# Batch 7's gate product in seven half-size products, and a new order of the work behind piece 340

## The chip, the cores and the metric

One core of one Trainium2 chip runs the whole program. The metric is the device time of one execution in microseconds. TensorE (PE, with its weight loads shown apart as PEld), VectorE (DVE), ScalarE (ACT) and GpSimd (POOL) each work through their own queue in order; SyncE (SP) issues the DMAs.

## What is computed

Per batch (8) and head (8) there are two attentions over 576 positions, one over means of four and one over a band of +-3, and their outputs are added. The 512-wide result x goes through a gated network:

```
h = gelu(x @ w_in)                     # 512 -> 1024
u, v = h[..., :512], h[..., 512:]
v_n = (v - mean) / sqrt(var + 1e-6) * g_ln
v_s = einsum('ts,bsd->btd', w_sg, v_n) + b_sg[None, :, None]
out = x + (u * v_s) @ w_out
```

## The kernel before

**Pieces and order.** The program is a list of small pieces, each with a name, the engines that can run it, what it comes after and which buffers it takes and gives back. The string ORDER names every piece in the order in which it is issued, with the engine behind a slash where there is a choice (A for ACT, V for DVE, P for POOL). So each engine's queue is written out by hand. `place` hands out the eight PSUM banks and the numbered SBUF buffers (10 of kind X, 38 of kind R) along that list; waits between engines follow from the data.

**Names.** The number behind an attention piece is the group g (batch x 4 + pair of heads, 0 to 31): YS scores, T, U and t the turning of probabilities, D the product with the values, xa, xb the merge, xh and xl the high and low part of x. In the network the first number is the batch: v7.3 is the third 128-position tile of the v half of batch 7 (12 matmuls; v7.4 is the left-over 64 positions, 8), vg its gelu, vb its statistics, vp the root on POOL, vn the normalising, vh and vl its high and low part. u is the other half (12 matmuls each), ua its gelu. s is the gate product, sa its scale and bias (DVE reads PSUM), sm the multiplication with u, ga to gd sums of gate blocks, gh and gl their high and low parts, o the out product, oa its addition to x, os the store.

**Numbers in two parts.** Each float32 operand is cut into a high part that the matmul takes exactly and a remainder. A product is three matmuls: high by high, low by high, high by low.

**The gate product before.** For each 128 columns of v_n and each half (288) of the output positions, `s_mm` adds 4 tiles of positions x 3 terms and 2 matmuls for the left-over 64, 14 in all; eight such pieces s7.0 to s7.7 make a batch. Each has a bank of its own and one sa reads it. From batch 1 on the out product is made with seven products of 6 matmuls instead of eight (`o_mm_s`, the Winograd form of Strassen's scheme), and several of them share a bank, which DVE reads in between.

**What ends the program.** The last pieces are out products of batch 7, their additions and eight half-block stores.

Of the kernel before, what the change touches and what calls it, by code (L numbers as in the profile page):

```python
# [1221 lines left out]
```

## Time and profile before

| | us |
|---|---|
| three timed runs | 565.53, 567.17, 568.70 (median 567.17) |
| the profiled execution | 564.37, its span 562.4 |
| PE busy | 546.4 (97%) |
| DVE, ACT, POOL busy | 437.2, 392.7, 364.1 |

The span runs from the first to the last instruction that the profiler saw. A matmul's end is modelled and matmuls overlap in the pipeline, so the mean length of one is longer than the distance to the next.

### The profile page before, as it was taken

To read this page: it belongs to the slowest core of one execution; us is meant where nothing else is said; L and a number is where in the kernel's file an instruction comes from. 1 tells how busy PE (TensorE), PEld (TensorE's weight loads), DVE (VectorE), ACT (ScalarE), POOL (GpSimd) and SP (SyncE) were. 2 spreads that over 40 slices of the span, in tenths; PEclk is the share of its full clock that TensorE was granted. 3 is DMA by queue.
4 is the path that set the end of the run, shared out by engine and by line. 5 is a ranking of instruction groups with operands and counts; after the bars stand their busy time and mean duration, and the time that the engine had idled before them with its cause. 6 is when DMAs were issued, how large, how long until landed. Compare 5 with 4: busy or idle time off the path is not lost.

```text
span 562.4 us, 17517 instructions
## 1 busy us (share of the span) xinstructions
PE 546.4 (97%) x6948; PEld 510.1 (91%) x6948; DVE 437.2 (78%) x929; ACT 392.7 (70%) x1302; POOL 364.1 (65%) x462
## 2 busy tenths in 40 slices
PE   6888999999999999999999999999999999999997
PEld 4677999799988999989999999989999899989997
DVE  7998899966889887796867867898669776565375
ACT  2897989779845989568987978377868588324310
POOL 6995987796776765747567645448655875655422
PEclk9998999999999999999999999999999999999999
DMA  8979551411623044041443124213353032200002
GB/s 290 289 237 339 196 179 40 121 45 37 204 82 121 23 140 157 16 153 55 135 124 105 46 83 152 77 55 105 108 172 102 11 113 78 99 1 0 32 34 105
DMA packets 31040, 62.72 MB, mean 112 GB/s; under 512 B 3696, under 2 KB 4720, under 8 KB 30960
## 3 DMA queue, kind: packets, MB, share of 16 engines
q1 hardware_dynamic: 30960, 61.62, 34.8%
q8 instruction: 54, 0.88, 0.7%
q14 instruction: 26, 0.21, 0.1%
...
## 4 chain that ended last, share of the span: by engine, by line
PE 79%; DVE 8%; ACT 4%; DMA 4%; POOL 3%; issue 2%; DVEq 0%; POOLq 0%; SPq 0%; ACTq 0%
PE ps L896 34%; PE ps L801 17%; PE ps L1019 14%; PE ps L677 3%; PE ps L693 2%; PE ps L616 2%; PE ps L625 2%; PE ps L514 2%; PE ps L535 2%; ACT X L574 2%; DMA R<-in_v_dram 2%; DMA R<-in_qT_dram 1%; DMA weight_z<-in_w_in_dram 1%; DVE vs L943 1%; POOL X L610 1%
## 5 line engine op out<-in xcount | busy, mean ns | idle before, releaser
L896 PE MATMUL ps<-wsg_h,R 128*128 128x288 f32 x576 | 122.6, 299 | 0.0
L896 PE MATMUL ps<-X,weight_z 128*128 128x288 f32 x512 | 110.8, 298 | 0.0
L801 PE MATMUL ps<-weight_y,X 128*128 128x512 f32 x320 | 98.1, 400 | 0.6 <-DVE vs L943 0.6
L574 ACT ACTIVATE X<-X,nb 128x64 f32<-128x64 f32 x280 | 93.6, 343 | 3.1 <-DVE nb L553 2.8
L896 PEld LDWEIGHTS ps<-wsg_h,R 128*128 128x128 f32 x576 | 93.8, 188 | 0.9
L896 PE MATMUL ps<-wsg_l,R 128*128 128x288 f32 x320 | 92.6, 295 | 0.0
L896 PEld LDWEIGHTS ps<-X,weight_z 128*128 128x128 f32 x512 | 84.6, 188 | 0.4
L896 PE MATMUL ps<-R,weight_z 128*128 128x288 f32 x256 | 75.4, 295 | 0.0
L801 PEld LDWEIGHTS ps<-weight_y,X 128*128 128x128 f32 x320 | 58.0, 189 | 12.4 <-DVE vs L943 1.2
L1026 DVE TENSOR_TENSOR R<-ps,R 128x288 f32<-128x288 f32 x98 | 43.0, 450 | 26.6 <-PE ps L1019 26.4
L896 PEld LDWEIGHTS ps<-wsg_l,R 128*128 128x128 f32 x320 | 60.3, 188 | 0.0
L244 ACT CAST R<-R 128x576 fp32r<-128x576 f32 (+2 forms) x65 | 41.5, 646 | 25.9 <-POOL R L949 10.1
L574 ACT ACTIVATION_READ_ACCUMULATOR X<-X,nb 128x1 f32 x280 | 54.5, 195 | 0.0
L1002 POOL TENSOR_TENSOR R<-R,R 128x576 fp32r<-128x576 f32 x23 | 35.2, 1531 | 27.5 <-ACT R L244 17.2
L949 POOL TENSOR_TENSOR R<-R,vs 128x288 f32<-128x288 f32 x29 | 24.8, 858 | 42.9 <-DVE vs L943 33.7
L1019 PE MATMUL ps<-R,weight_r 128*128 128x288 f32 x336 | 51.4, 297 | 0.0
L943 DVE SCALAR_TENSOR_TENSOR vs<-ps,g_sb,b_sb 128x288 f32<-128x288 f32 x64 | 32.5, 512 | 23.8 <-PE ps L896 20.9
L801 PE MATMUL ps<-weight_y,R 128*128 128x512 f32 x128 | 51.0, 398 | 0.0
L896 PEld LDWEIGHTS ps<-R,weight_z 128*128 128x128 f32 x256 | 48.2, 188 | 0.1
L1019 PEld LDWEIGHTS ps<-R,weight_r 128*128 128x128 f32 x336 | 46.8, 188 | 1.0
L498 POOL TENSOR_TENSOR pairs<-R 112x256 f32<-112x256 f32 x56 | 45.3, 809 | 3.3 <-DMA R<-in_v_dram 3.2
L244 ACT COPY R<-ps 112x288 f32<-112x288 f32 (+4 forms) x83 | 29.1, 391 | 17.6 <-PE ps L625 5.1
...
## 6 DMA issues: line engine op xcount, KB each, us to landing
...
```

The lines of the kernel that those rows point to most:

```text
L244: (nc.scalar.copy if e == "A" else ENG[e].tensor_copy)(**kw)
L498: ENG[e].tensor_tensor(out=pairs, in0=v[:, 0:2], in1=v[:, 2:4], op=ALU.add)
L514: nc.tensor.matmul(out=sp[i][os, c * KB:(c + 1) * KB], lhsT=q[hs, t * QB:t * QB + KB], rhs=k[hs, t * QB:t * QB + KB], start=not early, sto ...
L574: nc.scalar.activation(out=st["ms"][:, t, :], in_=src, func=AF.Exp, bias=st["nb"][:, t:t + 1], scale=scale, accum_out=sums[par][:, t:t + 1])
L677: nc.tensor.matmul(out=out, lhsT=lhsT, rhs=pdt[ks, probs, h * QC:(h + 1) * QC], start=first, stop=last)
L801: nc.tensor.matmul(out=acc, lhsT=r32(l), rhs=r32(weights[f"y{k}"][:, 0, w]), start=(i == 0 and ks[0] == 0), stop=(i == len(ops) - 1 and ks ...
L896: nc.tensor.matmul(out=acc[:, 0:HALF], lhsT=r32(l), rhs=r32(r), start=(first and n == 0), stop=(last and n == len(ops) - 1))
L943: nc.vector.scalar_tensor_tensor(out=vsb[i], in0=at["ps", "m", b, "s", i][:, 0:HALF], scalar=g_sb[:, i // 2:i // 2 + 1], in1=b_sb[:, half( ...
L949: ENG[e].tensor_tensor(out=gate(i), in0=gate(i), in1=vsb[i], op=ALU.mult)
L1002: ENG[e].tensor_tensor(out=r32(gl[m]), in0=us[raws[m]], in1=gh[m], op=ALU.subtract)
L1019: nc.tensor.matmul(out=bank(j, c), lhsT=r32(l), rhs=r32(r), start=first and i == 0, stop=i == len(ops) - 1, skip_group_check=not first)
L1026: nc.vector.tensor_tensor(out=x, in0=bank(j, c), in1=x, op=ALU.add)
```

## The change

The gate product of batch 7 (SMALL_S = 7) is made in the seven-product form too. The positions s are cut into two halves of two tiles, the columns of v_n into two halves of 256, the output positions into two halves of 288.

Weights: `gate_whole` adds the two parts of w_sg again (gf0 to gf4), `gate_combo` makes four differences of quarters (gx1 to gx4) and one of the left-over rows (gx5), `gate_split` cuts them into high (gy) and low (gz) parts. They go into six buffers of kind X (and a seventh for the left-over rows); the third overwrites the quarter of w_sg that no product uses any longer once the odd s pieces of batches 0 to 6 are done. v: eight pieces vc make sums of 128x256, and seven instead of four tiles are cut into vh and vl.

Products: for each j (two blocks of 128 columns) seven pieces s7.jn, n from 1 to 7. Each adds 2 tiles x 3 terms; n = 2, 3, 4 and 7 add two matmuls for the left-over positions. Pieces 1, 6, 7 and 4 follow one another in one bank, 5 and 3 in another, 2 has its own. Where a piece adds to what a bank holds, it comes after the sa that reads it. There are 14 sa; the second of a pair adds to what the first made.

Order: the first 340 names of ORDER stay; behind them all is written anew. Of the pieces that both lists have, 324 change engine. The list has 2324 names for 2278. The last lines for both, and the code:

```diff
...
-u7.7 vl7.3/P s7.0 s7.1 sa7.0 sm7.0/V oa6.04 sa7.1 s7.2 sa7.2 s7.3 sm7.2/P u7.6 oa6.06 sm7.1/P os6.1 s7.5 sa7.3 sm7.3/V
-ga7/V sa7.5 o6.17 sm7.5/P s7.7 sa7.7 gh7.3/V u7.4 ua7.7 gh6.6/A gl6.6/P oa6.12 sm7.7/V gb7/V gh7.0/A gh7.4/A gl7.3/V
-gc7/V gh7.5/V gl7.0/V s7.4 sa7.4 ua7.4 ua7.6 o6.07 gh7.2/A oa6.02 o6.14 oa6.13 s7.6 sm7.4/P gl7.2/V sa7.6 sm7.6/P
-gh7.1/A o7.01 oa7.00 o7.15 gd7/V gh7.6/A gl7.4/V o7.11 oa7.10 oa7.15 o7.05 oa7.05 o6.04 os6.0 os6.3 o7.06 o7.16 oa7.11
-oa6.03 o7.03 oa7.06 oa7.01 gl7.6/V os6.2 gl7.1/P o7.12 oa7.14 os7.1.0 o7.13 oa7.16 gl7.5/P o7.07 o7.17 os7.0.1 o7.02
-oa7.02 os7.1.1 oa7.12 os7.3.1 oa7.04 os7.0.0 os7.2.1 o7.04 oa7.03 os7.2.0 o7.14 oa7.13 os7.3.0
...
+gc6/V gb6/V gx4/V vp7.1 ua7.1 gd6/V gy5/V vg7.2 vb7.2/V xc31 gl6.1/V gh6.4/A vp7.2 v7.4 va7.4/V vj7.4 gz1/V vn7.2/V
+vn7.0/V gl6.4/V vg7.4 vn7.1/A vb7.4/A gz2/P vp7.4 o6.02 vc7.01/V vc7.02/V vc7.04/V gy4/A vh7.5/A gz5/V u7.6 u7.7
+vn7.4/A gh6.5/A v7.3 o6.12 oa6.04 oa6.10 vg7.3 vc7.03/P vb7.3/A vp7.3 u7.3 ua7.3 vn7.3/A u7.0 gl6.5/V oa6.00 o6.16
+vh7.4/V vl7.4/V o6.06 u7.4 vc7.11/P vc7.12/V oa6.11 oa6.01 vc7.14/P u7.5 oa6.14 vl7.5/V vh7.2/A vl7.2/V u7.2 vh7.6/A
+vl7.6/V gz4/V o6.17 gh6.3/A gl6.3/V ua7.4 vh7.3/A o6.07 s7.05 ua7.6 vl7.3/V s7.02 vh7.7/A vl7.7/V sa7.02 s7.03 vh7.0/A
+vc7.13/P ua7.0 vl7.0/V vh7.1/A vl7.1/V s7.01 sa7.00 o6.15 sa7.03 sa7.01 sm7.0/V s7.06 gh6.2/A gl6.2/V sa7.04 s7.15
+s7.07 ua7.5 oa6.12 s7.12 oa6.15 ua7.2 sa7.05 sm7.5/V s7.04 sa7.12 oa6.02 s7.13 sm7.1/P sa7.06 sm7.4/V sa7.10 gh6.6/A
+gl6.6/P s7.11 sa7.11 o6.13 s7.16 sa7.13 oa6.16 os6.1 sa7.14 sm7.3/V ua7.7 o6.05 oa6.05 s7.17 sa7.15 o6.03 s7.14
+sm7.2/P gh7.0/A sm7.7/V ga7/P gl7.0/V o7.01 o6.04 gh7.3/A gb7/V sa7.16 gh7.2/A gl7.3/V o7.11 oa6.03 o7.05 os6.2 o6.14
+sm7.6/P gh7.1/A oa7.00 gh7.4/A gd7/V gh7.6/A gl7.1/V gc7/V gl7.2/P gh7.5/A gl7.5/P gl7.4/V oa7.10 o7.02 oa7.04 os7.0.0
+o7.15 oa7.15 o7.06 o7.16 oa7.11 o7.13 oa6.13 os6.3 oa7.01 oa6.06 os6.0 o7.12 oa7.14 oa7.05 oa7.16 os7.1.1 o7.17 oa7.12
+o7.07 oa7.02 os7.2.1 os7.3.1 os7.1.0 o7.03 oa7.06 os7.0.1 gl7.6/P o7.14 oa7.13 os7.3.0 o7.04 oa7.03 os7.2.0
...
-EARLY_S, EARLY_D, WIDE, SMALL_O = 4, 4, 4, 1
+EARLY_S, EARLY_D, WIDE, SMALL_O, SMALL_S = 4, 4, 4, 1, 7
...
+    def gate_combo(m):
+        out, a, b = {1: (0, 1, 0), 2: (3, 3, 0), 3: (1, 3, 1), 4: (2, 2, 3)}[m]
+        part = lambda n: at["R", "wf", n][:, 0:S]
+        return lambda e: ENG[e].tensor_tensor(out=part(out), in0=part(a), in1=part(b), op=ALU.subtract)
...
+    def gate_split(m):
+        raw, pool = ("R", "wf", {1: 0, 2: 3, 3: 1, 4: 2, 5: 4}[m]), "X"
...
+        def high(e):
+            if m == 3:
+                gate_w[m] = [quarter(wsg_h, 1), quarter(wsg_l, 1)]
+            elif m == 5:
+                t = buf(pool, "wh", m)
+                gate_w[m] = [t[:, 0:HALF], t[:, HALF:S]]
+            else:
+                gate_w[m] = [pair_of(buf(pool, "wh", m))]
+            copy(e, out=r32(gate_w[m][0]), in_=source())
+
+        def low(e):
+            if m in (1, 2, 4):
+                gate_w[m].append(pair_of(buf(pool, "wl", m)))
+            h, l = gate_w[m]
+            ENG[e].tensor_tensor(out=r32(l), in0=source(), in1=h, op=ALU.subtract)
...
+    for n in range(NS):
+        add(f"gf{n}", {"P": 1.3, "V": 0.66}, gate_whole(n), ["wlq4"] if n == 4 else [f"wlq{n // 2 * 2}", f"wlq{n // 2 * 2 + 1}"],
+            takes=[("R", "wf", n)])
+    for m, after in ((1, ["gf0", "gf1"]), (3, ["gx1", "gf3"]), (2, ["gx1", "gx3"]), (4, ["gx2", "gf2"])):
+        add(f"gx{m}", {"P": 1.3, "V": 0.66}, gate_combo(m), after)
+    add("gx5", {"P": 0.8, "V": 0.4}, gate_diff, ["gf4"])
...
+        def v_sum(c, m):
...
+                lo, hi = slice(0, DM // 2), slice(DM // 2, DM)
+                near, far, x = vact[c][0], vact[2 + c][0], vraw[5 + c]
+                out, in0, in1, op = {1: (x[:, lo], far[:, hi], near[:, hi], ALU.add),
+                                     2: (x[:, hi], x[:, lo], near[:, lo], ALU.subtract),
+                                     3: (near[:, hi], near[:, lo], near[:, hi], ALU.subtract),
+                                     4: (vraw[7][:, hi if c else lo] if m == 4 else None, far[:, lo], x[:, hi], ALU.subtract)}[m]
+                ENG[e].tensor_tensor(out=out, in0=in0, in1=in1, op=op)
+            return emit
...
+        def s_left(n):
+            return [(0, 0), (0, 1), (1, 1), (1, 0)][(2, 3, 7, 4).index(n)]
+
+        def s_place(n, c):
+            return [(c, 0), (2 + c, 0), (7, c * 256), (2 + c, 256), (5 + c, 0), (5 + c, 256), (c, 256)][n - 1]
+
+        def s_rhs(n, c):
+            m = (0, 2, 3, "T4", "T1", "T2", "T3")[n - 1]
+            if type(m) is str:
+                return [t[:, c] for t in gate_w[int(m[1])]]
+            return [quarter(t, m)[:, c] for t in (wsg_h, wsg_l)]
...
+        def s_mm_s(j, n, bk, first):
...
+                ops = []
+                for c in range(2):
+                    k, col = s_place(n, c)
+                    ds = slice(col + j * P, col + (j + 1) * P)
+                    (vh, vl), (wh, wl) = vhat[k], s_rhs(n, c)
+                    ops += [(vh[:, ds], wh), (vl[:, ds], wh), (vh[:, ds], wl)]
+                if n in (2, 3, 7, 4):
+                    r, t = s_left(n)
+                    l = vhat[NS - 1][0][:, (2 * r + j) * P:(2 * r + j + 1) * P]
+                    cs = half(t)
+                    ops += [(l, w) for w in (gate_w[5] if n == 4 else [wsg_h[:, NS - 1, cs], wsg_l[:, NS - 1, cs]])]
+                for i, (l, r) in enumerate(ops):
+                    nc.tensor.matmul(out=s_bank(j, bk), lhsT=r32(l), rhs=r32(r), start=first and i == 0,
+                                     stop=i == len(ops) - 1, skip_group_check=not first)
+            return emit
...
+                i, v = (2 * r + j) * 2 + t, (vs2 + third[-1:])[{(0, 0): 0, (1, 1): 1, (0, 1): 2, (1, 0): 0}[r, t]]
+                vsb[i] = v
+                nc.vector.scalar_tensor_tensor(out=v, in0=s_bank(j, bk), scalar=g_sb[:, 2 * r + j:2 * r + j + 1],
+                                               in1=v if more else b_sb[:, half(t)], op0=ALU.mult, op1=ALU.add)
...
+            if small_s and not last:
+                continue
...
-        for i in range(2 * KT):
+        if small_s:
+            C = lambda c, m: f"vc{b}.{c}{m}"
+            for c in range(2):
+                after = {1: [N("vn", c), N("vn", 2 + c)], 2: [C(c, 1)], 3: [C(c, 1)], 4: [C(c, 2)] + ([C(0, 4)] if c else [])}
+                for m in (1, 2, 3, 4):
+                    add(C(c, m), {"P": 0.75, "V": 0.36}, v_sum(c, m), after[m],
+                        takes=[("R", "vx", b, c)] if m == 1 else [("R", "vx", b, 2)] if m == 4 and c == 0 else [])
+            high_after = ([C(0, 3)], [C(1, 3)], [N("vn", 2)], [N("vn", 3)], None, [C(0, 2)], [C(1, 2)], [C(1, 4)])
+            low_after = ([C(0, 2)], [C(1, 2)], [C(0, 1), C(0, 4)], [C(1, 1), C(1, 4)], None, [C(0, 4)], [C(1, 4)], [])
+            for k in (0, 1, 2, 3, 5, 6, 7):
+                add(N("vh", k), {"A": 0.58, "V": 0.35}, v_high_s(k), high_after[k], takes=[("R", "vh", b, k)])
+                add(N("vl", k), {"V": 0.62, "P": 1.25}, v_low_s(k), [N("vh", k)] + low_after[k], takes=[("R", "vl", b, k)],
+                    gives=[("R", "v", b, k) if k < 4 else ("R", "vx", b, k - 5)])
...
+                def prod(n, bk, after=(), first=False):
+                    ks = sorted({s_place(n, c)[0] for c in range(2)})
+                    left = n in (2, 3, 7, 4)
+                    w = [f"gz{m}" for m in range(1, 6)] + ["gy3"] if b <= SMALL_S + 1 and n in (4, 5, 6, 7) else []
+                    add(O(n), {"T": 1.08 if left else 0.81}, s_mm_s(j, n, bk, first),
+                        [N("vl", k) for k in ks] + ([N("vl", NS - 1)] if left else []) + w + list(after),
+                        takes=[key(bk)] if first else [],
...
+                def bias(n, r, t, bk, more, after, wait=(), last=False):
+                    add(A(n), {"V": 0.49}, s_bias_s(j, r, t, bk, more), [O(after)] + list(wait),
...
+                prod(2, "a", first=True)
+                bias(0, 0, 0, "a", False, 2, free(1, 0), last=True)
+                prod(1, "b", first=True)
+                bias(1, 0, 0, "b", True, 1, [A(0)])
+                prod(5, "e", first=True)
+                bias(2, 1, 1, "e", False, 5, free(1, 1))
+                prod(3, "e", [A(2)])
+                bias(3, 0, 1, "e", False, 3, free(0, 1), last=True)
+                prod(6, "b", [A(1)])
+                bias(4, 0, 1, "b", True, 6, [A(3)])
+                prod(7, "b", [A(4)])
+                bias(5, 1, 1, "b", True, 7, [A(2)])
+                prod(4, "b", [A(5)])
+                bias(6, 1, 0, "b", False, 4, [sm(0, 0)], last=True)
+                for r, t, n in ((0, 0, 1), (0, 1, 4), (1, 1, 5), (1, 0, 6)):
+                    i = (2 * r + j) * 2 + t
+                    add(N("sm", i), {"V": 0.46, "P": 0.83}, s_gate(i), [A(n), N("ua", i)],
+                        gives=[("X", "vs", b)] if (r, t, j) == (0, 1, 1) else [])
+        for i in range(0 if small_s else 2 * KT):
...
```

## Rows read from the trace of the kernel before

**Rows 1.** The page: the span, and busy time, share of the span and instructions of each engine.

```profile
span 562.4 us, 17517 instructions
PE 546.4 (97%) x6948; PEld 510.1 (91%) x6948; DVE 437.2 (78%) x929; ACT 392.7 (70%) x1302; POOL 364.1 (65%) x462
```

**Rows 2.** Busy time by stretch, up to the end of the first 340 pieces and after. Columns: stretch in us and its length; for PE, PEld, DVE, ACT and POOL the busy time (and instructions); the granted TensorE clock; the DMA share; GB/s.

```profile
0.00:70.00 70.00, 60.19 (x1081) 49.74 (x1082) 62.04 (x144) 53.09 (x182) 55.99 (x72) 0.95 0.85 271
70.00:562.40 492.40, 486.20 (x5869) 460.31 (x5867) 375.17 (x786) 339.63 (x1121) 308.09 (x390) 1.00 0.29 89
```

**Rows 3.** The chain that ended last, from 525 us to the end. Columns: start in us, length in us, what, and how many instructions are merged.

```profile
524.98 12.44 PE ps L896 x94
545.11 1.86 PE ps L896 x14
546.96 11.94 PE ps L1019 x90
```

**Rows 4.** The timeline, its last instruction before the last store lands: start, length, engine, line, what, count, and in brackets the idle time before it and what ended that.

```profile
558.93 0.46 DVE L1026 TENSOR_TENSOR R<-ps,R 128x288 f32<-128x288 f32 x1 [0.33 <-PE ps L1019]
```

**Rows 5.** Busy time by stretch, as in rows 2, finer.

```profile
100.00:120.00 20.00, 19.40 (x210) 15.77 (x212) 16.48 (x30) 14.91 (x57) 16.17 (x18) 1.00 0.24 70
140.00:160.00 20.00, 18.75 (x334) 18.24 (x333) 15.82 (x29) 16.81 (x52) 14.19 (x15) 1.00 0.58 186
160.00:180.00 20.00, 19.24 (x226) 17.79 (x225) 19.89 (x35) 8.35 (x34) 15.79 (x19) 1.00 0.33 101
200.00:450.00 250.00, 250.00 (x3134) 236.19 (x3137) 196.28 (x422) 190.87 (x637) 152.19 (x203) 1.00 0.33 100
450.00:546.00 96.00, 96.00 (x913) 92.69 (x907) 57.07 (x124) 45.59 (x128) 52.31 (x66) 1.00 0.15 49
```

**Rows 6.** Waits of PE from 70 us on: who waited for whom; us in total, times, longest.

```profile
PE ps L677 <- DVE R L244: 1.2, 1, 1.2
PE ps L801 <- DVE vs L943: 0.6, 1, 0.6
PE ps L625 <- POOL pd L613: 0.6, 1, 0.6
```

**Rows 7.** Groups of instructions by line from 494 us to the end (the last two rows keep shapes apart). Columns: line, engine, operation, out<-in, shapes, count; busy us, mean ns of one; idle before, and for whom.

```profile
L896 PE MATMUL ps<-wsg_h,R 128*128 128x288 f32 x82 | 17.2, 295 | 0.0
L1026 DVE TENSOR_TENSOR R<-ps,R 128x288 f32<-128x288 f32 x28 | 12.1, 452 | 10.1 <-PE ps L1019 10.0
L1002 DVE TENSOR_TENSOR R<-R,R 128x576 fp32r<-128x576 f32 x8 | 6.1, 773 | 0.0
L949 POOL TENSOR_TENSOR R<-R,vs 128x288 f32<-128x288 f32 x7 | 5.6, 810 | 17.7 <-DVE vs L943 15.8 <-ACT R L924 2.0
L943 DVE SCALAR_TENSOR_TENSOR vs<-ps,g_sb,b_sb 128x288 f32<-128x288 f32 x10 | 5.2, 516 | 11.0 <-PE ps L896 9.7 <-POOL R L949 1.3
L865 ACT ACTIVATE R<-R,nm,rs 128x512 f32<-128x512 f32 (+1 forms) x5 | 3.9, 809 | 4.9 <-POOL nm L855 4.9
L990 DVE TENSOR_TENSOR R<-R,R 128x576 f32<-128x576 f32 x5 | 3.8, 755 | 0.4 <-POOL R L949 0.3
L854 POOL TENSOR_TENSOR rs<-rs,nhalf 128x1 f32<-128x1 f32 (+1 forms) x5 | 3.6, 727 | 2.9 <-DVE rs L844 2.7
L817 ACT ACTIVATE R<-ps 128x512 f32<-128x512 f32 x4 | 2.4, 597 | 12.8 <-PE ps L801 12.8
L949 DVE TENSOR_TENSOR R<-R,vs 128x288 f32<-128x288 f32 x4 | 1.8, 456 | 0.2
L855 POOL TENSOR_SCALAR nm<-mv,rs 128x1 f32<-128x1 f32 (+1 forms) x5 | 1.6, 319 | 0.5
L838 ACT ACTIVATE squares<-R,mv 128x512 bf16<-128x512 f32 (+1 forms) x2 | 1.4, 724 | 0.1
L853 POOL TENSOR_SCALAR rs<-rs 64x1 f32<-64x1 f32 (+1 forms) x2 | 0.7, 328 | 1.2 <-ACT squares L838 1.1
L837 ACT ACTIVATE mv<-sum_all 128x1 f32<-128x1 f32 (+1 forms) x2 | 0.4, 196 | 0.0
L817 ACT ACTIVATION_READ_ACCUMULATOR R<-ps 128x1 f32 x1 | 0.2, 195 | 0.0
L244 DVE CAST R<-R 128x576 fp32r<-128x576 f32 x7 | 5.0, 718 | 0.1
L887 DVE TENSOR_TENSOR R<-R,R 128x512 fp32r<-128x512 f32 x1 | 0.7, 684 | 0.0
```

**Rows 8.** Groups by line and shape over the whole run, columns as in rows 7.

```profile
L949 DVE TENSOR_TENSOR R<-R,vs 128x288 f32<-128x288 f32 x35 | 22.5, 643 | 0.5
L1026 DVE TENSOR_TENSOR R<-ps,R 128x288 f32<-128x288 f32 x98 | 43.0, 450 | 26.6 <-PE ps L1019 26.4
L924 ACT ACT_TABLE_LOAD x14 | 18.0, 1283 | 2.8 <-PE ps L896 2.5
```

**Rows 9.** The chain that ended last, from 446 us, columns as in rows 3.

```profile
445.91 1.86 PE ps L801 x8
448.57 0.56 PE ps L677 x15
449.13 0.53 PE ps L693 x34
```

**Rows 10.** Waits of PE's weight loads from 70 us on, columns as in rows 6.

```profile
PEld ps L677 <- issue: 4.2, 15, 1.5
```

More of the change, by code (lines that the diff above doesn't have):

```diff
@@ L445, with quarter, pair_of, gate_whole @@
         w_sg(s)
+    gate_w = {}
+    def quarter(t, n):
+        return t[:, n // 2 * 2:n // 2 * 2 + 2, n % 2 * HALF:(n % 2 + 1) * HALF]
+    def pair_of(ap):
+        return ap[:, 0:S].rearrange("p (a b) -> p a b", a=2)
+    def gate_whole(n):
+        def emit(e):
+            if n == 4:
+                out, h, l = buf("R", "wf", n)[:, 0:S], wsg_h[:, n, :], wsg_l[:, n, :]
+            else:
+                out, h, l = pair_of(buf("R", "wf", n)), quarter(wsg_h, n), quarter(wsg_l, n)
+            ENG[e].tensor_tensor(out=out, in0=h, in1=l, op=ALU.add)
+        return emit
@@ new lines, in gate_combo, with gate_diff, source @@
+    def gate_combo(m):
+        out, a, b = {1: (0, 1, 0), 2: (3, 3, 0), 3: (1, 3, 1), 4: (2, 2, 3)}[m]
+        part = lambda n: at["R", "wf", n][:, 0:S]
+        return lambda e: ENG[e].tensor_tensor(out=part(out), in0=part(a), in1=part(b), op=ALU.subtract)
+    def gate_diff(e):
+        f = at["R", "wf", 4]
+        ENG[e].tensor_tensor(out=f[:, 0:HALF], in0=f[:, 0:HALF], in1=f[:, HALF:S], op=ALU.subtract)
+    def gate_split(m):
+        raw, pool = ("R", "wf", {1: 0, 2: 3, 3: 1, 4: 2, 5: 4}[m]), "X"
+        def source():
+            return at[raw][:, 0:HALF] if m == 5 else pair_of(at[raw])
+        def high(e):
[4 more added lines that the diff above has]
+                gate_w[m] = [t[:, 0:HALF], t[:, HALF:S]]
+            else:
+                gate_w[m] = [pair_of(buf(pool, "wh", m))]
[5 more added lines that the diff above has]
+            ENG[e].tensor_tensor(out=r32(l), in0=source(), in1=h, op=ALU.subtract)
+        plain = [f"s{b}.{i}" for b in range(SMALL_S) for i in range(1, 8, 2)] if m == 3 else []
+        add(f"gy{m}", {"A": 0.58, "V": 0.4}, high, [f"gx{m}"] + plain, takes=[] if m == 3 else [(pool, "wh", m)])
+        add(f"gz{m}", {"P": 1.3, "V": 0.66}, low, [f"gy{m}"] + {1: ["gx2"], 2: ["gx4"]}.get(m, []),
+            takes=[(pool, "wl", m)] if m in (1, 2, 4) else [], gives=[raw])
@@ L448 @@
+    for n in range(NS):
[4 more added lines that the diff above has]
+    add("gx5", {"P": 0.8, "V": 0.4}, gate_diff, ["gf4"])
+    for m in range(1, 6):
+        gate_split(m)
     sts = [[dict() for _ in range(NPAIR)] for _ in range(NB)]
@@ new lines, in v_high_s, with emit, v_low_s @@
+        def v_high_s(k):
+            def emit(e):
+                vhat[k] = [buf("R", "vh", b, k), None]
+                copy(e, out=r32(vhat[k][0][:, 0:DM]), in_=vact[k][0] if k < 4 else vraw[k])
+            return emit
+        def v_low_s(k):
+            def emit(e):
+                vhat[k][1] = buf("R", "vl", b, k)
+                ENG[e].tensor_tensor(out=r32(vhat[k][1][:, 0:DM]), in0=vact[k][0] if k < 4 else vraw[k],
+                                     in1=vhat[k][0][:, 0:DM], op=ALU.subtract)
+            return emit
```

221 lines of the change are left out of this document (123 added, 98 removed).

## The prediction

> **What bounds it now.** I began with the page: PE is busy for 546.4 of 562.4 us and DVE, the next, for 437.2, ACT for 70% of the span [rows 1]. Next the stretches: up to 70 us PE lacks 9.8 us of work, at a granted clock of 0.95 (1.00 after), and that stretch belongs to the first 340 pieces, which the change leaves alone. From 70 us on it is busy 486.20 of 492.40 us [rows 2]. Of the 6.2 us missing, 3.5 lie after the last matmul: it ends at 546.96 + 11.94 = 558.9 [rows 3], one addition on DVE follows, then the last store [rows 4]. So 2.7 us of idle are left in between, and the finer stretches put them at 100 to 120 us (0.60), 140 to 160 (1.25) and 160 to 180 (0.76); from 200 to 450 none [rows 5]. The waits of PE name 2.4 us of that [rows 6]. The chain of waits in the last 37 us is PE alone [rows 3]. So this kernel is a queue of matmuls, and a change is worth the matmuls that it takes out, plus or minus the idle that it removes or makes.
>
> **Matmuls removed.** Batch 7's gate product was eight pieces of 14 matmuls, 112. After, each of two column blocks j has seven products of 6 (two tiles of s, three terms), and four carry two more for the 64 left-over rows: 2 x (42 + 8) = 100. Ninety-four matmuls of L896 take 12.44 us, a piece of 14 takes 1.86 [rows 3]: 0.133 us each, whether 14 or 6 share a bank (the out products, in sixes, take 11.94/90). 12 x 0.133 = **-1.6 us**. Every other product keeps its count (6948 becomes 6936).
>
> **Preparation on other engines.** Added are 20 pieces for combined weights (gf, gx, gy, gz), 8 differences of v (vc), three more high and three more low splits, six more bias steps (14 for 8). By the engines in the new order DVE gets: eight sums of 576 columns at 0.755 and one of 288 at 0.456 (6.5), the casts gy1, gy2, gy5 (about 1.8), the remainders gz1 and gz4 at 0.773 and gz5 (2.0), four vc at 0.456 (1.8), six more vl at 0.684 (4.1), six sa at 0.516 (3.1), two more sm (0.9) [rows 7]: 20 us. From 450 to 546 us DVE is busy for 57.1 of 96 us [rows 5]; 77 fit. POOL gains about 2 us net and ACT 3. The weights' work, some 10 us of DVE, stands between D29 (467.7 us in the old order) and u7.6; all but gz4 is listed 18 us of matmuls ahead of its first reader, s7.05. I cost it at nothing: PE's own queue of that stretch hides it. Without that cover the end would move by what was late, at most those 10 us; a gain is excluded, since it only adds.
>
> **The way into the product.** In the old order PE does 17.7 us of other work between v7.3 (ends 508.7) and s7.0 (526.4); in the new one 90 matmuls, 11.9 us. What must fit: gelu 0.60 and its sum 0.20; statistics 0.20 + 0.72 + 0.19; three small POOL steps 0.33 + 0.73 + 0.32; normalising on ACT 0.81; vc7.11 on POOL 0.81; vc7.12 on DVE 0.46; three additions and three low splits queued on DVE, 1.36 + 2.05 [rows 7]. That is 8.8 us and some eight hand-overs, 0.1 us or less each. Over two us spare: **0**.
>
> **Reads between products of a bank.** New are eight places where a product waits until DVE has read what its bank held (s7.x3, x6, x7, x4, for both j). Behind a waiting product stands all of PE's queue. A matmul runs 0.295 us where the next starts after 0.13 [rows 7], so some 0.16 passes after the last one's turn, then the bias step's 0.516: about 0.7, with two semaphores 0.75 to 0.8. The order puts one piece of 6 (0.80) or 8 (1.06) between, or more. For s7.07 the DVE queue counts too. Behind vc7.12, which ends 5.4 us after v7.3 by the sum above, it holds three additions (1.36), seven low splits vl (4.79), gz4, gl6.3 and gl6.2 (2.32), five sa (2.58) and sm7.0 (0.46): 11.5 us, so sa7.04, the last, could end at 16.9; PE reaches s7.07 at 11.9 + 5 x 0.80 + 2 x 1.06 = 18.0. Bounds: 0 if all is covered; 8 x 0.78 = 6.2 if none is. Nearest the cover that is listed: 0.05 each at five tight places, **+0.25**.
>
> **Behind the last piece.** Before, o7.06 (its low part waits for gd7) stood five products, 30 matmuls and 4.0 us, behind s7.6, with sa7.6, sm7.6 on POOL, gd7 and gl7.4 in between, 0.52 + 0.81 + 0.76 + 0.77 = 2.9, and PE did not wait. Now o7.02 stands as far behind s7.14, and DVE must do sa7.16, gl7.3, two additions, gd7 and gl7.1 first: 0.52 + 0.77 + 0.90 + 0.76 + 0.77 = 3.7, plus 0.16, and the rest of gb7, up to 0.7 [rows 7]. **+0.35**, between 0 and 0.8. The end (last addition, half-block store) stays as it is.
>
> A rule of the Trainium skill speaks against DVE's part: SBUF — State Buffer, "SBUF: two separate sides", has a DVE operation with two SBUF inputs and a GpSimd operation exclude one another for a whole instruction. The trace agrees in direction: the gate multiplication of 128x288 took 0.643 us on DVE in the mean of the run and 0.456 in the last 68 us, where POOL works less, while an addition that reads PSUM took 0.45 in both [rows 7, 8]. By the rule vc7.11, 7.14 and 7.13, 0.81 each on POOL, could push the 16.9 above to 19.3, and the sum would be 1.3 us higher.
>
> **The rest of the order.** From 70 us on everything is rearranged: 324 pieces common to both change engine. The bounds are the 2.7 us of idle, which a better order would recover, and a like amount or a few us more, which a worse one would make. The two lists, with rates of the trace (0.13 us per 288-column matmul, 0.23 per 512-column one, about 1.1 for a D) [rows 3, 9], say little: PE work between scores (YS) and turning (T), groups 5 to 31, rises from 21 to 23 us in the mean and from 10.6 to 15.7 in the least; between T and the D that needs it the mean falls from 7.6 to 5.6, the least stays 1.9. ACT changes its table 52 times for 50, 2 x 1.28 us [rows 8], on an engine with 30% to spare [rows 1]. I take **0**.
>
> **Sum.** -1.6 + 0.25 + 0.35 = -1.0 us. The profiled execution took 564.37 us for a span of 562.4, so 563.4 on its scale. It lies under the fastest of the three timed runs (565.53, median 567.17), so against the median: **566.2 us**, -0.2%. A measurement here can tell about 0.5%, 2.8 us, from no change: under 564.3 is faster, over 570.0 slower.
>
> **Rivals.**
> *The new order also fills the holes* (chance 0.30). The 2.6 us between 100 and 180 us go as well: -3.6, 563.6. For it: those holes are short waits for DVE and POOL [rows 6], and the YS-to-T distance got longer just where they were. Against: the engines are as full as before there (DVE 19.89 of 20 at 160 to 180 [rows 5]), and T to D got shorter.
> *DVE sets the pace in the new product* (0.09), slower. If DVE is more than about a microsecond later than its queue sum at s7.07, each product of a bank waits for its read: 8 x 0.78 = 6.2, net 567.17 - 1.6 + 6.2 + 0.35 = 572.1. For it: 14 reads for 8 and a queue with no gap. Against: the queue sum ends before PE arrives.
> *PE starves before the D products* (0.10), slower. PE's weight loads already wait 4.2 us in 15 places ahead of L677 [rows 10]; with the shorter cover from T to D these double: -1.0 + 4.2, 570.4. It decides where T to D falls near the copies' length. Against: much of that wait is for issue, which an order hardly alters, and the least cover did not shrink.
> *It does not do what it says*: if pieces of six cost PE more each than pieces of fourteen, the saving is gone, 567.2 + 0.6. The out products contradict it; I give it 0.01 and count it with the forecast, which it leaves within 0.5%.
>
> **Chances and range.** Forecast 0.51, within 0.5%; filled holes 0.30, faster; both slow rivals and the like, 0.19. The range goes from 562.5 (matmuls and all idle, and some spread of the runs) to 570.5, which takes in the starving D and leaves out the paced product; the forecast's own is 564.4 to 568.5.
>
> **What would show it.** Matmuls 6936. Right: PE's idle from 70 us to its last matmul between 2 and 4 us, the s7 pieces (100 matmuls and the few between) without a wait over 0.2 us, o7.02 waiting a few tenths. Wrong: PE waiting for the bias step at many places, or for L677 over 6 us in total; PE idle under 1 us would be the first rival.

## The result: 3.4 us slower, and the profile after

Over eight runs of each the changed kernel takes 569.45 us in the median (568.61 to 572.51), the kernel before 566.01 (563.64 to 568.70): ratio 1.0071, 95% interval 1.0048 to 1.0093. The forecast was 566.2, no change. The time lies in the range, near its upper end; the sign was missed. The forecast started from 567.17, the median of three runs, which the median of eight puts 1.2 us lower: from the base the forecast was -1.0 us and the measurement +3.4.

Below, the page, the stretches as in [rows 2, 5], and the waits of PE and of its weight loads from 70 us on, as in [rows 6, 10]. The profiled execution took 570.7 us. Lines of kernel.py have moved: L677 is now L742, L896 is L1036 (batch 7's gate product L1016, its bias step L1026), L949 is L1089, L990 is L1130, L1002 is L1142, L1019 is L1159, L1026 is L1166, L244 is L247.

```profile
span 568.9 us, 17556 instructions
PE 549.1 (97%) x6936; PEld 511.6 (90%) x6936; DVE 451.0 (79%) x941; ACT 411.8 (72%) x1339; POOL 356.1 (63%) x469
```

```profile
70.00:568.90 498.90, 489.19 (x5871) 461.66 (x5869) 390.11 (x802) 359.98 (x1163) 302.31 (x399) 1.00 0.28 88
...
140.00:160.00 20.00, 20.00 (x280) 19.61 (x282) 16.96 (x34) 14.02 (x54) 16.58 (x18) 1.00 0.48 156
...
200.00:450.00 250.00, 246.44 (x3215) 231.86 (x3218) 189.50 (x394) 192.54 (x647) 157.80 (x212) 1.00 0.34 104
```

```profile
PE ps L742 <- DVE R L247: 1.9, 2, 1.7
PE ps L742 <- ACT nb L616: 1.0, 1, 1.0
PE ps L1159 <- DVE R L1142: 0.8, 1, 0.8
PE ps L1036 <- DVE R L765: 0.8, 1, 0.8
...
PEld ps L742 <- issue: 6.0, 19, 1.9
```

The 6936 matmuls are there. The holes of the old order at 100 to 120 (20.00 busy now too) and 140 to 160 us are filled; in exchange the stretch from 200 to 450 us, full before, lacks 3.6 us. PE's waits, with three small ones at L1159 (1.0 us together) that are left out here, sum to 5.5 us, where [rows 6] names 2.4. None of them is at L1016.

For the sum I measure from the first matmul of v0.3, where the first 340 pieces end on PE (70.0 us before, 71.8 after; that start differs between runs of one kernel too), to the end of the last matmul (558.9 and 564.7). That is 488.9 us before and 492.9 after, **+4.0**. There is one profile of each kernel, but where two lists agree their stretches agree too: from v0.3 to D28 it is 378.5 us before and 378.6 to 378.8 in the four runs below that keep that part as it was. A piece's length is taken from its first matmul to that of the next piece. Then the eight pieces s7 of before take 14.83 us, the fourteen of after 13.69: **-1.1**. The other pieces cost **+5.1**: less the median of pieces of the same kind and length, +3.2 of it lies ahead of D28 (448 us) and the remaining 1.9 behind it. Over 0.9 us late start s0.2 (at 84 us, 0.99), D14 (1.09) and D15 (1.81), and o7.02 ends 1.05 late; smaller ones are o2.02, o2.12, YS26 and o5.12 (0.4 to 0.6 each).

**D15 and D14.** The timeline of after, instructions of ACT, DVE, POOL and PE around the two (start, length, engine, line, what, count, idle before and its end):

```profile
207.14 0.44 DVE L765 TENSOR_TENSOR R<-ps,od 128x290 f32<-128x290 f32 x1
207.61 2.23 DVE L952 TENSOR_TENSOR R<-R,R 64x512 fp32r<-64x512 f32 x1
...
210.23 0.63 DVE L247 COPY R<-ps 128x464 f32<-128x464 f32 x1
...
207.59 0.46 POOL L564 TENSOR_TENSOR vd<-pairs 112x128 f32<-112x128 f32 x1
208.01 1.28 POOL L952 TENSOR_TENSOR R<-R,R 128x512 fp32r<-128x512 f32 x1
...
212.35 0.56 PE L742 MATMUL ps<-R,vd 48*64 48x144 f32 x14 [0.95 <-ACT nb L616]
...
224.47 1.28 ACT L1064 ACT_TABLE_LOAD   x1
225.76 1.01 ACT L1064 ACTIVATE R<-ps 128x288 f32<-128x288 f32 x3
226.65 0.72 ACT L247 COPY R<-ps 128x464 f32<-128x464 f32 x2
...
227.41 0.72 DVE L247 COPY R<-ps 112x288 f32<-112x288 f32 x2 [4.95 <-ACT R L247]
...
228.01 0.58 PE L742 MATMUL ps<-R,vd 48*64 48x144 f32 x14 [1.65 <-DVE R L247]
```

Ahead of D14, DVE's low split vl2.4 (64x512) takes 2.23 us; a split of twice as many partitions took 0.684 in [rows 7]. It starts 0.02 us after a step on POOL and ends 0.55 us after a second one, queued right behind, is over (209.29). The additions around it, which read PSUM, take their usual 0.44 to 0.46. The copies that D14 needs stand behind it, the last of them on ACT behind one of DVE's. Ahead of D15 there is no such thing: the new order puts the copies pa15 and pb15 on ACT, behind a table load and three gelus (2.3 us), while DVE, which makes the third copy, has been idle for 4.95 us.

**The tail.** DVE's groups from 496 us to the end, as in [rows 7], and the timeline around o7.02:

```profile
L1130 DVE TENSOR_TENSOR R<-R,R 128x576 f32<-128x576 f32 x7 | 7.6, 1100 | 0.0
...
L1026 DVE SCALAR_TENSOR_TENSOR vs<-ps,g_sb,vs 128x288 f32<-128x288 f32 x4 | 2.1, 518 | 1.7 <-PE ps L1016 1.7
```

```profile
553.50 1.97 DVE L1130 TENSOR_TENSOR R<-R,R 128x576 f32<-128x576 f32 x1
555.40 0.74 DVE L1142 TENSOR_TENSOR R<-R,R 128x576 fp32r<-128x576 f32 x1
...
553.43 1.43 POOL L1142 TENSOR_TENSOR R<-R,R 128x576 fp32r<-128x576 f32 x1
...
556.20 1.33 PE L1159 MATMUL ps<-R,weight_r 128*128 128x288 f32 x8 [0.79 <-DVE R L1142]
```

The sum gd7 on DVE takes 1.97 us, not 0.755: POOL started gl7.2 0.07 us ahead of it, and gl7.2 takes 1.43. gl7.1 (L1142), the low part that o7.02 waits for, follows. In the groups the seven sums of L1130 have a mean of 1.100 us for 0.755 before, while L1026, a bias step that reads PSUM, takes 0.518 for 0.516.

**One of the small ones, o5.12.** DVE and PE around it:

```profile
472.06 4.12 DVE L464 TENSOR_TENSOR R<-wsg_h,wsg_l 128x576 f32<-128x576 f32 x1
476.10 0.45 DVE L1166 TENSOR_TENSOR R<-ps,R 128x288 f32<-128x288 f32 x1
...
476.60 1.06 PE L1159 MATMUL ps<-R,weight_r 128*128 128x288 f32 x6 [0.38 <-DVE R L1166]
```

The first line is gf4, a step of the product's preparation. It takes 4.12 us, while POOL works through a row of steps from 471.1 to 476.5 us; the addition behind it on DVE is what o5.12 waits for.

### The profile page after: what moved, and what is told of

It reads as the page before. It is cut to its first block, busy times and chain, and to the rows that moved or that the text cites. A ratio compares the mean times of both kernels' runs of the same rounds, so it can differ in the third digit from the quotient of the medians.

```text
span 568.9 us, 17556 instructions
## 1 busy us (share of the span) xinstructions
PE 549.1 (97%) x6936; PEld 511.6 (90%) x6936; DVE 451.0 (79%) x941; ACT 411.8 (72%) x1339; POOL 356.1 (63%) x469
## 4 chain that ended last, share of the span: by engine, by line
PE 83%; DVE 7%; ACT 5%; issue 3%; DMA 2%; SPq 0%; DVEq 0%; ACTq 0%
PE ps L1036 34%; PE ps L866 18%; PE ps L1159 12%; PE ps L742 4%; PE ps L758 3%; PE ps L579 3%; PE ps L600 3%; PE ps L681 2%; PE ps L690 2%; PE ps L1016 2%; DMA weight_y<-in_w_in_dram 1%; ACT X L639 1%; ACT R L247 1%; ACT pd L661 1%; DMA R<-in_qT_dram 1%
## 5 line engine op out<-in xcount | busy, mean ns | idle before, releaser
L1036 PE MATMUL ps<-X,weight_z 128*128 128x288 f32 x512 | 111.2, 300 | 0.0
L1036 PE MATMUL ps<-wsg_h,R 128*128 128x288 f32 x504 | 108.1, 301 | 0.8 <-DVE R L765 0.8
L1036 PEld LDWEIGHTS ps<-X,weight_z 128*128 128x128 f32 x512 | 84.5, 188 | 0.8
L1036 PEld LDWEIGHTS ps<-wsg_h,R 128*128 128x128 f32 x504 | 81.8, 188 | 2.0 <-issue 1.0
L1036 PE MATMUL ps<-wsg_l,R 128*128 128x288 f32 x280 | 81.0, 295 | 0.0
L1036 PE MATMUL ps<-R,weight_z 128*128 128x288 f32 x256 | 75.5, 295 | 0.0
L247 ACT CAST R<-R 128x576 fp32r<-128x576 f32 (+2 forms) x77 | 48.6, 645 | 20.9 <-POOL R L1089 5.5
L1166 DVE TENSOR_TENSOR R<-ps,R 128x288 f32<-128x288 f32 x98 | 41.3, 450 | 22.2 <-PE ps L1159 21.8
L1036 PEld LDWEIGHTS ps<-wsg_l,R 128*128 128x128 f32 x280 | 52.7, 188 | 0.0
L1089 POOL TENSOR_TENSOR R<-R,vs 128x288 f32<-128x288 f32 x31 | 29.0, 937 | 37.8 <-DVE vs L1083 29.6
L1159 PE MATMUL ps<-R,weight_r 128*128 128x288 f32 x336 | 50.7, 298 | 1.7 <-DVE R L1142 0.8
L1159 PEld LDWEIGHTS ps<-R,weight_r 128*128 128x128 f32 x336 | 46.6, 188 | 3.6 <-DVE R L1142 1.0
L1036 PEld LDWEIGHTS ps<-R,weight_z 128*128 128x128 f32 x256 | 48.2, 188 | 0.2
L247 DVE COPY R<-ps 128x464 f32<-128x464 f32 (+4 forms) x61 | 26.5, 453 | 18.6 <-ACT R L247 10.2
L678 POOL TENSOR_TENSOR pd<-pd,rc 128x432 f32<-128x432 f32 x24 | 23.4, 976 | 26.8 <-DVE rc L672 26.8
L1064 ACT ACTIVATE R<-ps 128x288 f32<-128x288 f32 x64 | 24.8, 410 | 19.3 <-PE ps L1036 11.1
```

The source lines that it names most:

```text
L247: (nc.scalar.copy if e == "A" else ENG[e].tensor_copy)(**kw)
L678: ENG[e].tensor_tensor(out=st["pdv"], in0=st["pdv"], in1=bc_last(bc_last(st["rc"][:, NT:], 3), QC), op=ALU.mult)
L1036: nc.tensor.matmul(out=acc[:, 0:HALF], lhsT=r32(l), rhs=r32(r), start=(first and n == 0), stop=(last and n == len(ops) - 1))
L1064: nc.scalar.activation(out=gate(i), in_=at["ps", "m", b, "u", i][:, 0:HALF], func=AF.Gelu_apprx_tanh)
L1089: ENG[e].tensor_tensor(out=gate(i), in0=gate(i), in1=vsb[i], op=ALU.mult)
L1159: nc.tensor.matmul(out=bank(j, c), lhsT=r32(l), rhs=r32(r), start=first and i == 0, stop=i == len(ops) - 1, skip_group_check=not first)
```

## The experiments

The two theories were: the new order, ahead of D28 and in the tail, makes the waits and the product is worth its matmuls; or the product with its preparation is what costs. Each time stands beside that of the kernel before, taken in the same rounds. "Stretch" is from v0.3 to the last matmul in its profile, against the 488.9 us of before.

### The old order up to D28 (e1_product), the new one up to D28 (e2_order)

```diff
...
-vb6.0/V xc27 pe28/V vb6.1/V vp6.1 vp6.0 oa5.06 D28 YS30 oe28/A vb6.2/V vp6.2 my30 lq31 od28 lw29 xa28 lk31 lw30 lv29
+vb6.0/V xc27 pe28/V vb6.1/V vp6.1 vp6.0 oa5.06 D28 lw29 oe28/A vb6.2/V YS30 ma30 od28 rc29 xa28 my30 u6.4 ny30/A vp6.2
...
```

The diff is e1's, against the order of before: up to D28 nothing changes, behind it stand the remaining names in the new order, with the seven products. e2 is the reverse: the new order up to D28, then the remaining names in the old one with the old product, whose form needs no combined weights. In e2's lines below the numbers are one higher than before's (L245 for L244).

> The old order up to D28 (449 us), then the changed kernel's order with its seven products. Theory A (the loss is mostly the new order ahead of D28: waits of PE at s0.2, D14, D15, o2.02, o2.12 that the old order had not, about 3 us more than the old order's own): PE has 2.7 us of named idle or less up to 449 us as before, and the stretch behind D28 costs -1.6 for the matmuls, +1.0 at o7.02 and about +1 besides: 566 to 568 us where before is 566. Theory B (the seven products' stage itself costs the 4 us): 569.5 to 570.5, as the changed kernel.

> The new order up to D28, then the old order with the old gate product of eight pieces. The pieces of the combined weights are left out, they belong to the product. Theory A: the waits at s0.2, D14, D15, o2.02 and o2.12 stand in the trace as in the changed kernel, and the time is 568.5 to 570 us, 2.5 to 4 above before. Theory B: 565 to 567, no change from before, since what was rearranged is equally good.

Measured: e1 570.33 us for 565.44, ratio 1.0081 (1.0051 to 1.0112), stretch 491.9; e2 571.43, 1.0101 (1.0069 to 1.0133), stretch 495.9. Both are slower than before, and e1's time falls where the second theory had it, e2's above what the first one said. But each seam makes waits of its own, in e1 D29 2.26 us late and u6.4 0.57, in e2 two of 1.68 and 1.31. Without these the stretches would be, by estimate, 489.1 and 492.9, those of before and of after. The places say the same. Waits of PE in e2, and its timeline ahead of D15:

```profile
PE ps L678 <- DVE R L245: 1.9, 2, 1.7
...
PE ps L678 <- ACT nb L552: 0.9, 1, 0.9
...
PE ps L897 <- DVE R L701: 0.7, 1, 0.7
```

```profile
223.71 0.72 DVE L245 COPY R<-ps 112x288 f32<-112x288 f32 x2 [4.95 <-ACT R L245]
```

With the old product and none of its preparation, s0.2 (1.00 late), D14 (1.09), D15 (1.81) and o2.12 (0.63) are late by the same amounts as in after, DVE's 4.95 us of idle included; in e1 none of them is. They belong to the order. In e1 the s7 pieces show no wait either.

### The tail (e3_tail, e4_product_tail)

```diff
...
-gl7.1/V gc7/V gl7.2/P gh7.5/A gl7.5/P gl7.4/V oa7.10
+gl7.1/V gc7/V gh7.5/A gl7.5/P gl7.4/V gl7.2/V oa7.10
...
```

One name, gl7.2, goes from POOL to DVE, behind gl7.4; e3 is after with it, e4 is e1 with it.

> The changed kernel with one piece moved: gl7.2 from POOL to DVE, behind gl7.4. Theory C (gd7 took 1.97 us and not 0.75 on DVE because gl7.2 on POOL, started 0.07 us earlier, held it off until it ended; that, not DVE's queue, made PE wait at o7.02): gd7 takes 0.75 us, the wait of about 1 us at o7.02 is gone or under 0.2, 1.0 us less than the changed kernel: 568.4. Rival (DVE's queue of sa7.16, gl7.3, additions, gd7, gl7.1 is too long by itself, as the prediction's term of 0.35 had it): the wait stays at 0.4 us or more, 569 us.

> The old order up to D28, the seven products behind it, and gl7.2 on DVE behind gl7.4. If theories A and C hold together: 565 to 566.5 us, at or a little under before (matmuls -1.6, no wait at o7.02, what else waits behind D28 about +1). If B holds: 568.5 or more.

Measured: e3 569.20, 1.0060 (1.0040 to 1.0079), stretch 492.0, 0.9 less than after; e4 571.03, 1.0077 (1.0047 to 1.0108), stretch 491.2. e3's timeline:

```profile
551.00 0.76 DVE L1130 TENSOR_TENSOR R<-R,R 128x576 f32<-128x576 f32 x1
...
548.78 5.19 PE L1159 MATMUL ps<-R,weight_r 128*128 128x288 f32 x38
```

gd7 is back at 0.76 and PE runs 38 matmuls without a wait; 0.29 is left later, ahead of o7.16. The mechanism is shown in the profile. From the start of s7.14 to the last matmul it is worth 0.65 us (15.05 to 14.40, and 14.79 in e1 to 14.14 in e4); the rest of e3's gain comes from D14, which did not wait there: with the same list, vl2.4 met only the end of POOL's split and took 0.98 us, and T14 waited 0.6 in its place. So whether two steps meet depends on tenths of a microsecond.

In the medians 0.65 us is under what the interval resolves, and e4's median, again where the second theory had it, is higher than its stretch (+2.3 us on before, where the medians say +5.6). The record has the mean granted clock of each execution: 0.996 in e4's profiled one, the fastest, and 0.984 to 0.990 in seven of the eight others. Its median execution (0.987) lost 0.009 of 569 us more to the clock, by estimate 5 us, and is 4.7 longer. Where the clock was low in it, and whether this kernel has a part in that, is not on record.

### The product in the old order (e5_product, e6_product_late)

```diff
...
-t30 s6.0 sa6.0 pb30/V u6.4 ua6.4 ua6.6 xh29/A pc30/A s6.5 T31 U31 t31 pe30/A s6.3 D30 oe30/V lv31 os5.2 lw31 sm6.1/P
+u6.4 ua6.4 u6.6 ua6.6 os5.2 os5.1 xh29/A xl29/V s6.0 sa6.0 t30 sa6.1 pb30/V pc30/V gf3/V gf0/V u6.7 xl28/V gx1/V gx5/V
+gx3/V s6.2 pe30/A D30 lv31 sm6.1/V oe30/V od30 xa30 xb30 ua6.2 sm6.0/V s6.5 U31 t31 s6.3 sa6.3 T31 sa6.2 lw31 xc29
...
```

The seam is moved to a quieter place. e5 keeps the old order up to s6.1 (473 us), with gf4 and gf1 set in, and is new from there; e6 keeps it up to D31 (486 us), with the ten weights' pieces that come first set in. Both have the mended tail.

> The old order up to s6.1 (473 us), only gf4 and gf1 of the weights set into it, then the changed kernel's order with the seven products and gl7.2 on DVE. The two earlier splices had waits at their seam (2.3 and 0.6 us; 1.7 and 1.3 us), which this one should not have. Theory A (the product is worth its matmuls and its stage costs little; the loss is the new order's waits and the blocked gd7): no single wait of PE over 0.3 us behind s6.1, and 0.5 to 1.5 us under before. Theory B (the stage itself costs more than it saves): 1 us or more over before, with the lost time spread between 500 and 560 us.

> As the last, but the old order runs up to D31 (486 us) and ten of the weights' pieces are set into it behind the neighbours that they have in the new order; then the new order, gl7.2 on DVE. Theory A: the same as the last within 0.5 us, since the pieces for the weights lie in DVE's free time. Theory B': these pieces delay others on DVE, and PE waits 1 us or more between 473 and 500 us.

Measured: e5 566.90 for 566.35, 1.0013 (0.9983 to 1.0043), stretch 490.0; e6 571.36, 1.0089 (1.0057 to 1.0120), stretch 494.9. Neither came out as the first theory had it. e5 has one wait behind its seam, 1.47 us ahead of s6.3; e6 loses 6.9 us at three places around D31. e5's timeline, DVE, POOL and PE:

```profile
484.01 0.75 DVE L777 TENSOR_TENSOR R<-R,X 128x576 fp32r<-128x576 f32 x1
484.68 0.75 DVE L470 TENSOR_TENSOR R<-R,R 128x576 f32<-128x576 f32 x1
485.35 0.45 DVE L474 TENSOR_TENSOR R<-R 128x288 f32<-128x288 f32 x1
485.72 0.75 DVE L470 TENSOR_TENSOR R<-R,R 128x576 f32<-128x576 f32 x1
486.39 0.45 DVE L1089 TENSOR_TENSOR R<-R,vs 128x288 f32<-128x288 f32 x1
...
487.66 0.83 DVE L765 TENSOR_TENSOR R<-ps,od 128x290 f32<-128x290 f32 x2
...
483.97 4.13 POOL L464 TENSOR_TENSOR R<-wsg_h,wsg_l 128x576 f32<-128x576 f32 x1 [2.23 <-PE ps L742]
...
488.27 0.50 PE L1036 MATMUL ps<-wsg_h,R 128*128 128x288 f32 x2 [1.24 <-DVE R L765]
```

s6.3 needs the bank that xb30 (L765) reads, and xb30 stands behind DVE's weights' steps. And in e6, POOL's step, the D that waits for it, and the stretch in which the clock was low (columns as in [rows 2]):

```profile
487.51 1.12 POOL L563 TENSOR_TENSOR pairs<-R 112x256 f32<-112x256 f32 x1 [3.48 <-DMA R<-in_v_dram]
...
488.75 1.17 PE L742 MATMUL ps<-R,vd 48*64 48x144 f32 x16 [3.48 <-POOL pairs L563]
490.44 1.34 PE L758 MATMUL ps<-R,X 64*64 64x58 f32 x40 [0.52 <-DMA X<-in_vw_dram]
```

```profile
487.50:494.40 6.90, 5.14 (x67) 4.50 (x68) 5.62 (x7) 0.62 (x2) 4.64 (x5) 0.51 0.32 94
```

Here the sums took R buffers early, so the load of batch values for D31 (lv31) was handed the buffer that D30 gave back just before; SP's queue shows 4.7 us of wait for PE's L742 ahead of that load. Not all of the 6.9 us is waiting. PE stood idle from 485.3 us on, and at 487.5 its granted clock fell from 1.00 to 0.51, the lower of its two levels (1.2 for 2.4 GHz), for 6.9 us; matmuls of 288 columns then started 0.24 us apart, not 0.13. By the pieces' lengths 4.2 us are the two waits and 2.7 the matmuls at that clock. In the other profiles the clock is 1.00 from 70 us to the last matmul. So the preparation cost little by its own length in these runs, and a good deal by what it held up: a bank in e5, a buffer in e6.

### Mending (e7_mended, e8_best, e9_sums_behind, e10_all_mended)

e7 is after with three places mended, the tail as in e3 and

```diff
...
-lk17 vl2.4/V lw14 ec15 U14 u2.3 t14 ua2.3 xb13 vh2.3/A T14 u2.2 ua2.2 pa14/V mx15 pb14/V pc14/A
+lk17 lw14 ec15 U14 u2.3 t14 ua2.3 xb13 vh2.3/A T14 u2.2 ua2.2 pa14/V mx15 pb14/V vl2.4/V pc14/A
...
-pa15/A os0.1 t15 pb15/A pc15/V
+pa15/V os0.1 t15 pb15/V pc15/V
...
```

> The changed kernel with four pieces altered: pa15 and pb15 on DVE and not on ACT (where they stood behind a table load and three gelus), vl2.4 on DVE behind pb14 and not ahead of xb13 (it took 2.23 us and not 0.69 because GpSimd operations held it off), gl7.2 on DVE behind gl7.4. Theory A: the waits at D15 (1.8 us), D14 (1.1) and o7.02 (1.05) go to under 0.3 each, 3 to 4 us less than the changed kernel: 565.5 to 566.5, as before. Rival: PE only waits at the next place, and the gain is under 1.5 us.

Measured: 567.21 for 566.35, 1.0020 (0.9991 to 1.0049), stretch 489.7. Its timeline:

```profile
209.20 0.68 DVE L952 TENSOR_TENSOR R<-R,R 64x512 fp32r<-64x512 f32 x1
...
224.60 0.71 PE L742 MATMUL ps<-R,vd 48*64 48x144 f32 x12
```

vl2.4 takes 0.68 and D15 starts without a wait: three edits of order and engine, with no change in what PE computes, take 3.2 us off the stretch of after and bring it back to the time of before. The time, 0.7 us over what was expected, can't be told from before's. The waits that e7 leaves alone (s0.2, o2.02, o2.12, YS26, o5.12) stand as they were, and no run tries what makes them.

The other three go from e5. e8 moves pb11 and pe11 from ACT to DVE, where the old order has D15's trouble at D11 (before, ACT, DVE and PE):

```profile
154.46 1.28 ACT L924 ACT_TABLE_LOAD   x1
155.76 0.71 ACT L924 ACTIVATE R<-ps 128x288 f32<-128x288 f32 x2
...
156.65 0.46 DVE L244 COPY R<-ps 112x288 f32<-112x288 f32 x1 [2.80 <-ACT R L244]
...
157.25 0.56 PE L677 MATMUL ps<-R,vd 48*64 48x144 f32 x14 [1.25 <-DVE R L244]
```

```diff
...
-pb11/A pc11/V pe11/A vs11 D11
+pb11/V pc11/V pe11/V vs11 D11
...
```

> The product in the old order as in e5, and pb11 and pe11 on DVE and not on ACT: in the old order D11 waited 1.34 us because pb11 stood on ACT behind a table load and two gelus while DVE was idle. If the cause is that, the wait at D11 goes to under 0.2 us and the time is 1.3 us under that of e5, 1.5 to 3 us under before: 562.5 to 564. If D11 waits for something else (the loads of v), nothing changes.

e9 moves four weights' steps behind xb30:

```diff
...
-pc30/V gf3/V gf0/V u6.7 xl28/V gx1/V gx5/V gx3/V s6.2 pe30/A D30 lv31 sm6.1/V oe30/V od30 xa30 xb30 ua6.2
+pc30/V gf3/V u6.7 xl28/V s6.2 pe30/A D30 lv31 sm6.1/V oe30/V od30 xa30 xb30 gf0/V gx1/V gx5/V gx3/V ua6.2
...
```

> e8_best with four of the weights' steps on DVE (gf0, gx1, gx5, gx3) moved behind xb30 in the list. In e8_best PE waits 1.2 us for DVE's xb30 ahead of s6.3 (a bank that xb30 gives back), 1.47 us over the usual distance between pieces, while DVE works through those steps and those listed with them. My theory (a weights' step costs nothing unless something that gives back a bank or a buffer stands behind it on DVE): the wait ahead of s6.3 goes, no new one over 0.3 us comes, the stretch from D28 to the end falls by 1.2 to 1.5, and the time by the same: ratio to before about 0.995. Rival 1 (the steps are simply more work than DVE has room for there): a wait of about 1 us comes at another place between D30 and D31 or ahead of s7.05, and the time stays at e8_best's. Rival 2 (POOL is the limit, by operations that DVE holds off): the wait ahead of s6.3 stays.

e10 issues u1.5 ahead of t9:

```diff
...
-sm0.7/V v1.3 nq9/P t9 U9 lk12 ks12/V qs11/V xa8 wbr0 mx10 nx10/A vs9 wlr2/P T9 wtr0 pa9/V pb9/V pc9/V u1.5
+sm0.7/V v1.3 u1.5 nq9/P t9 U9 lk12 ks12/V qs11/V xa8 wbr0 mx10 nx10/A vs9 wlr2/P T9 wtr0 pa9/V pb9/V pc9/V
...
```

> e9_sums_behind with u1.5 issued ahead of t9 in place of behind T9 (its place is 21 names further on in the order of before). PE waits 0.8 us there between v1.3 and t9, for two operations that stand one behind the other on POOL. If that wait is only a matter of what PE has to do meanwhile, 14 matmuls of u1.5 cover it: it falls from 0.8 to under 0.2 and the time by 0.6 to 0.8, ratio to before about 0.994. Rival: what u1.5 no longer covers (T9 to D9, or ACT's gelu of u1.5 ahead of pa9's copies) costs as much as was gained, a new wait of 0.5 or more between T9 and D9, and the time is that of e9_sums_behind within 0.3.

| | us | ratio to before (95%) | stretch, us |
|---|---|---|---|
| e5_product | 566.90 | 1.0013 (0.9983 to 1.0043) | 490.0 |
| e8_best | 564.89 | 0.9982 (0.9950 to 1.0015) | 488.0 |
| e9_sums_behind | 563.19 | 0.9966 (0.9946 to 0.9985) | 486.8 |
| e10_all_mended | 562.47 | 0.9941 (0.9922 to 0.9959) | 486.3 |

e8 lies 0.9 us over what was expected of it. Each edit took the wait at which it was aimed: D11 in e8, s6.3 in e9 (0.35 came back ahead of s6.4), t9 in e10. e10's gain of 0.5 us in the stretch is a little less than the 0.6 to 0.8 that was expected; no wait came between T9 and D9. All that is left of PE's waits from 70 us on in e10, and its stretch from there to the last matmul:

```profile
PE ps L866 <- DVE vs L1083: 0.3, 1, 0.3
```

```profile
70.00:558.00 488.00, 487.51 (x5872) 461.37 (x5871) 397.13 (x824) 349.24 (x1142) 300.37 (x387) 1.00 0.29 88
```

e10 computes the seven products and beats both kernels: 3.3 us (0.6%) under before and some 7 under after. But most of this is not the product's. From v0.3 to D28, where neither the product nor its preparation stands, the stretch falls from 378.5 us before to 376.3, by the names moved at D11 and t9, which the kernel before could have too; no run tries them there alone. Behind D28, where the product and all its preparation lie, it is 110.4 before, 111.2 in e5 and 109.9 in e9 and e10: there the change is worth 0.45 us.

## Why the prediction was wrong

**What bounds it: right.** A queue of matmuls, worth its matmuls plus or minus the idle that it makes. Every gain and loss in the stretches above is that, but for the 2.7 us of e6 in which PE worked at the lower clock.

**Matmuls (-1.6) and reads between products (+0.25): right.** Together -1.35; the s7 pieces show -1.1 in after, e9 and e10 alike. No product waits over 0.2 us for its read. A matmul of the new product takes 13.69/100 = 0.137 us of PE's queue, of the old one 14.83/112 = 0.132, 0.45 us in all. It sits in the first matmul of s7.06, s7.07, s7.16, s7.17 and s7.14, behind which the next starts after 0.21 to 0.22 us and not 0.13. These are five of the eight places with a read, so this is what the reads cost, for the 0.25 of the sum. The rival in which DVE sets the pace there is out.

**The way into the product (0): right**, no wait there in after.

**Preparation at nothing: nearly right in after, by the place it had.** DVE's four sums gf took 6.3 us there and not 4 x 0.755, and PE's queue hid all but the wait of 0.4 to 0.5 us behind gf4, ahead of o5.12. But its price without cover was put as its own length, at most 10 us of DVE; e5 and e6 show that the price is that of the bank or the buffer that stands behind it: 1.5 us of PE in e5, 4.2 in e6 and there 2.7 more at the lower clock.

**Behind the last piece (+0.35): right place, wrong reason.** It measured 1.05, over the upper bound of 0.8. DVE's queue, which the term was worked out from, makes no wait at o7.02 by itself: in e3 it is as long and PE does not wait. The price that was wrong is that of gd7, 0.76 in the sum, which took 1.97. The sum counted what is queued on DVE ahead of o7.02 and took each length from the mean of a group; it didn't look at what POOL does in that moment, and gl7.2/P stands right behind gd7 in the list.

**The rest of the new order (0): this step failed, and with it the sign.** Its bounds (2.7 us either way or a few more) held the 3.2 us ahead of D28; the value was chosen at 0 because two mean distances in the lists moved in opposite directions. A mean says nothing here: the loss is in a handful of places. At the two that e7 frees, worth 2.6 us together from D13 to YS17 (26.7 to 24.1), what decides is who stands directly ahead of the copies for a D on ACT and on DVE, and both mechanisms could be read in the trace of before: D11 in the fence above, and v1.3, which starts 0.57 us late; in DVE's queue ahead of the step that frees its bank stands this gate multiplication, which takes 2.85 us, not 0.456, while POOL works through a row of steps up to 105.6 us:

```profile
103.09 2.85 DVE L949 TENSOR_TENSOR R<-R,vs 128x288 f32<-128x288 f32 x1
...
100.80 2.80 POOL L712 TENSOR_TENSOR R<-R,X 128x576 fp32r<-128x576 f32 x2
103.56 0.79 POOL L949 TENSOR_TENSOR R<-R,vs 128x288 f32<-128x288 f32 x1
104.32 1.30 POOL L366 TENSOR_TENSOR R<-R,weight_r 128x512 int32<-128x512 int32 x1
```

Searching the new list for these two patterns (a table load and gelus ahead of pa or pb on ACT; a two-input step on DVE with POOL steps beside it and a D's copies behind it) points at D14, D15 and gd7 before any run; how long each is held off it can't tell, as D14 in e3 shows.

**The rivals.** Nearest is "PE starves before the D products", priced 570.4 for a measured 569.45, and the sign set for a wrong forecast (over 6 us at this line) was just reached by the weight loads, which waited 6.0 us for issue, and not by PE itself with 2.9 at L742. But its reason, a shorter cover from T to D everywhere, isn't what happened: two D of 27 wait, and e7 frees both without changing their cover of matmuls. "The new order fills the holes" was half right: the holes at 100 to 160 us did go, and others came.

The Trainium skill's rule that the prediction weighed (SBUF — State Buffer, "SBUF: two separate sides": a DVE operation with two SBUF inputs and a GpSimd operation that reads SBUF exclude one another for a whole instruction) agrees with gd7 (1.97 for 0.755), vl2.4 (2.23 for 0.68), gf4 (4.12 for 0.755) and, the other way round, with gf2 on POOL (4.13 for 1.43). The prediction applied it to the three vc7 steps on POOL ahead of the product, where no wait came.
